# The order list of a three-stage token-mixing kernel, made anew

## The chip, the cores and the metric

The kernel runs on one core of one Trainium2 chip. The metric is the device time of one execution in microseconds. The kernel before takes 290.33 us (median of 3 runs, 290.14 to 290.52).

## The reference

Three layers follow one another on 2 batches of 768 tokens with 512 features, in float32; some weights come as 8-byte floats.

1. Retention attention, 8 heads of 64 features: for each block of tokens, `intra = (q k^T * Dmask) v`, `inter = (q * lam_pow) kv_state`, and then `kv_state = lam_block * kv_state + (k * rev_pow)^T v`.
2. A channel mix: `xk` and `xr` are mixes of each token with the one before it; `k = relu(xk @ w_k)` (512 to 1024), `v = k*k @ w_v`, `r = sigmoid(xr @ w_r)`, and the result is `r * v`.
3. A gated convolution: `gate = sigmoid(sum of 5 shifted, scaled copies of x)`, `val = x @ w_val`, and the output is `(gate * val) @ w_out`.

## The kernel before, in words

All tiles hold 128 partitions. Attention works on 12 chunks of 128 tokens (6 per batch). The two matrix layers work on three passes of 512 tokens (two groups of 256); in every product the operands are split into a high and a low part, and three matmuls (high-high, high-low, low-high) are summed in PSUM. TensorE does all products, VectorE (DVE) and ScalarE (ACT) evict, mix and split, GpSimd (POOL) takes some elementwise work, and SyncE (SP) issues the loads and stores.

Every piece of work is a named operation: `S8` is the scores of chunk 8, `U8` its key-value product, `M8` the masking of the scores on DVE, `N8.0` and `N8.1` the additions to the running state on DVE, `O8.0` and `O8.1` the decay of the state that goes ahead of them, `Y8` and `Z8` the products that make the output, `X8` its eviction. `k1.6.0` is the first half of the sum for row block 6 in pass 1 of the `w_k` product; `r`, `v`, `a` (`w_val`) and `p` (`w_out`) are named alike. `q0`, `k0`, `v0` are loads of tokens, `w0` to `w19`, `y0` to `y3` and `z0` to `z3` loads of weights, and letters behind these (`w3a` to `w3l`) the steps that make two float32 parts of an 8-byte weight.

Nothing plans the work when the kernel is built: one text, `ORDER` (lines 22 to 95), lists all operations, and each is issued in that order on its engine. A letter behind a colon (`:V`, `:A`, `:G`) names another engine than the usual one. An engine does its own operations strictly in the order of the list, and a wait stops all that stands behind it on that engine. A wait is put in where an operation touches what an operation ahead of it in the list has written or read, so the list decides not only when an operation comes, but also for which others it waits.

One PSUM tile matters here, `su`, two banks of 512 columns (line 203). From chunk 4 on, scores and state products share both banks: columns 0 to 255 of each hold what `S` writes and `M` reads, columns 256 to 511 what `U` writes and `N` reads, the first bank for `N.0`, the second for `N.1`:

```
su = psp.tile([P, 2, 512], F32, name="su")                      # line 203
su[half[j], s, Q * n:Q * n + Q]        # S, a matmul, line 571 (Q is 64, s the bank)
su[:, :, 0:NPAIR * Q]                  # M, on DVE, line 578 (NPAIR is 4)
su[half[s], j, c0:c0 + D]              # U, a matmul, line 592 (c0 is 256 + 64 n, j the bank)
u = su[:, j, NPAIR * Q:]               # N, on DVE, line 616
```

`Y` and `Z` are at line 655, all products at 754 and 942. In the trace the 16 or 32 matmul records of an `S` or a `U` stand as one row (`PE su L571`, `PE su L592`); `state` at L616 is an `N`, `b_M` at L578 an `M`.

Of the kernel before, what the change touches and what calls it, by code (L numbers as in the profile page):

```python
# [18 lines left out]


ORDER = """
    zero table eye lam scan warm7 w3 w3b w3a w3c w3d w3e w1 w2 w1a w2a q0 Tq0 w1b warm3 w3f:V
    w3h k0 w1c w1d w2c Tk0 k1 w1e w2d w0 Eq0:A w1f:V kd0 w2b Tk1 w2e w3l:V w2f:V Ek0:A D0:V
    warm2 w0a w0b v0 S0 q1 U0 w1h D1:V w2h k2 N0:A Tq1 w0c q3 pows:G Ek1:A Eq1:A w0d w0e w0f:G
    Tk2 M0 w1l:V S1 Q1 w2l:V Ek2:A D2:G M1 q2 quar Z0 Tq2 O1:V w0h Eq2:A w0l:V Q2 Tq3 Eq3:A Q3
    v1 k3 X0:A U1 N1 S2 Tk3 kd1 Z1 Ek3:A D3:G w4 M2 O2:V w4a X1:A S3 mu w4b muT H0 H1:G w4c
    w4d w4e w4f:G v2 muc mr0.1.0a:A mr0.3.0a:A U2 M3 N2 k4 Tk4 w4h mr0.1.0b mr0.0.0a:A O3:V
    mr0.2.0a:A q4 Z2 X2:A Tq4 mr0.1.0h w4l:V mr0.0.0b v3 mr0.3.0b w5 mr0.2.0b U3 N3 Eq4:A D4:V
    O4.0:V Ek4:A mr0.0.0h mr0.1.0l:V v4 mr0.0.0l:V mr0.3.0h mr0.3.0l:V Z3 Q4 w5a S4 X3:A w5c
    U4 N4.0 O4.1:G r0.00.0 M4 mk0.3a:A mr0.3.1a:A mr0.3.1b k5 Tk5 q5 mr0.1.1a:A Tq5 w5d  # L30
    r0.01.0 mr0.1.1b w5b mr0.0.1a:A mr0.2.0h mr0.0.1b w5e Eq5:A mr0.2.0l:V mk0.0a:A Ek5:A
    mr0.2.1a:A cw0 mk0.0b D5:G mk0.1a:A Y4 mr0.0.1h w7 w7a S5 r0.01.1 N4.1 mr0.1.1h M5
    mr0.2.1b mr0.3.1h mk0.1b w5f:V r0.00.1 mr0.1.1l:V mr0.0.1l:V w6 w6a mr0.3.1l:V w5h w6c w10
# [24 lines left out]
    k1.4.1 k1.5.1 mr1.1l:G k1.2e:V mr1.2a:A O10.0:V k1.2h N10.0 O10.1:G N10.1 Q10:V M10 k1.6.1
    X9:V k11 D11:V k1.1q:V z3 mr1.2b mr1.2h mr1.2l:G r1.3.0 k1.0q:V x1.3:A v11 Y10 S11 k1.4e:A
    k1.4h Z10 X10:A U11 x1.2:A k1.7h mr1.3h O11.0:V N11.0 M11 k1.6e:A k1.1l:V mr1.3l:G k1.6h  # L60
    r1.1.0 k1.2q:V z0 k1.5e:A Y11 Z11 X11:V H5:G r1.2.0 mk2.0a:V x3 mk2.0b r1.2.1 mk2.0h
    r1.3.1 k1.0l:V mk2.1a:V mk2.1b k1.3h k1.3q:A k1.4q:G r1.2s r1.1.1 r1.1s v1.3.0 r1.3s y0
    r1.0.0 r1.0.1 mk2.3a:A v1.0.0 k1.2l:G k1.3l:V v1.3.1 k1.4l:G mk2.2a:V k1.5h y0a mk2.2b
# [1030 lines left out]
```

## Time and profile before

| what | value |
|---|---|
| median of 3 runs | 290.33 us |
| the profiled execution | 290.39 us |
| its span, first to last instruction | 288.6 us |
| PE busy | 275.2 us, 95% |
| DVE busy | 235.4 us, 82% |
| ACT busy | 164.1 us, 57% |
| POOL busy | 49.3 us, 17% |
| granted TensorE clock | 1.000 |

The chain of waits gives PE 90% of the span, DMA 5%, DVE 3%. Busy PE is a modelled figure: matmuls overlap, and the step from one start to the next is what counts. The profiled execution is 1.8 us longer than its span.

### The profile page before, as it was taken

How to read it: one execution, taken by the hardware profiler on the slowest of the kernel's cores; microseconds unless marked ns; L12 is line 12 of the kernel's file. 1: busy time of each engine (PE TensorE's matmuls, PEld its weight loads, DVE VectorE, ACT ScalarE, POOL GpSimd, SP SyncE). 2: the span in 40 equal slices, each digit the busy share in tenths (PEclk: the TensorE clock that was granted, in tenths of full speed). 3: DMA queues.
4: the chain of work that ended last, by engine and by line, in shares of the span. 5: the costliest groups of instructions: out<-in, count | busy, mean ns of one | idle time of the engine just before them, and what ended most of it. 6: DMA issues, size and time to landing. Idle time of an engine off the chain costs nothing.

```text
span 288.6 us, 5971 instructions
## 1 busy us (share of the span) xinstructions
PE 275.2 (95%) x2345; PEld 229.1 (79%) x2345; DVE 235.4 (82%) x402; ACT 164.1 (57%) x309; POOL 49.3 (17%) x59
## 2 busy tenths in 40 slices
...
DMA packets 63626, 29.25 MB, mean 101 GB/s; under 512 B 58322, under 2 KB 58606, under 8 KB 63598
## 3 DMA queue, kind: packets, MB, share of 16 engines
...
q14 instruction: 10, 0.08, 0.1%
HBM read 25.72 MB, written 3.15 MB: 100 GB/s over the span
## 4 chain that ended last, share of the span: by engine, by line
PE 90%; DMA 5%; DVE 3%; ACT 1%; issue 1%; SPq 0%; DVEq 0%; ACTq 0%
PE b_k L754 23%; PE b_v L754 23%; PE b_r L754 12%; PE b_p L942 11%; PE b_a L754 11%; PE xx L655 4%; DMA b_v<-in_v_dram 2%; DMA xx<-in_moe_w_r_dram 2%; PE su L592 2%; PE su L571 1%; PE su L494 1%; PE xx L553 1%; PE b_Tq L440 1%; DVE xx L342 0%; DVE b_k L480 0%
## 5 line engine op out<-in xcount | busy, mean ns | idle before, releaser
L894 DVE SCALAR_TENSOR_TENSOR b_g<-xx,cw,b_g 128x512 f32<-128x512 f32 x48 | 38.5, 810 | 0.6
L754 PE MATMUL b_k<-b_mk_2h,w_rk 128*128 128x512 f32 x48 | 19.0, 397 | 0.0
L754 PE MATMUL b_r<-b_mr_0h,w_rk 128*128 128x256 f32 (+1 forms) x80 | 19.0, 312 | 0.0
L754 PE MATMUL b_k<-b_mk_0h,w_rk 128*128 128x512 f32 x48 | 18.9, 394 | 0.0
L754 PE MATMUL b_k<-b_mk_3h,w_rk 128*128 128x512 f32 x48 | 18.7, 390 | 0.0
L754 PE MATMUL b_k<-b_mk_1h,w_rk 128*128 128x512 f32 x48 | 18.7, 390 | 0.0
L902 ACT ACTIVATE b_g<-b_g 128x512 f32<-128x512 f32 x12 | 7.4, 628 | 16.6 <-DVE b_g L894 16.5
L754 PEld LDWEIGHTS b_r<-b_mr_0h,w_rk 128*128 128x128 f32 x80 | 13.2, 191 | 0.9
L869 DVE TENSOR_TENSOR xx<-b_v,xx 128x512 f32<-128x512 f32 x12 | 8.0, 687 | 6.4 <-PE b_v L754 6.4
L754 PE MATMUL b_r<-b_mr_0l,w_rk 128*128 128x256 f32 (+1 forms) x40 | 12.2, 305 | 0.0
L616 DVE TENSOR_TENSOR state<-su,state 128x256 f32<-128x256 f32 x13 | 5.5, 424 | 6.4 <-PE su L571 3.6
L754 PEld LDWEIGHTS b_k<-b_mk_2h,w_rk 128*128 128x128 f32 x48 | 9.0, 188 | 2.0
L754 PEld LDWEIGHTS b_k<-b_mk_0h,w_rk 128*128 128x128 f32 x48 | 9.0, 188 | 1.9
L754 PEld LDWEIGHTS b_k<-b_mk_3h,w_rk 128*128 128x128 f32 x48 | 9.0, 188 | 1.9
L754 PEld LDWEIGHTS b_k<-b_mk_1h,w_rk 128*128 128x128 f32 x48 | 9.0, 188 | 1.9
L440 PE MATMUL b_Tq<-ident,b_q 128*128 128x128 f32 x24 | 4.3, 309 | 5.6 <-DMA b_q<-in_q_dram 5.6
L754 PE MATMUL b_v<-b_k_0h,w_v 128*128 128x512 f32 x24 | 9.6, 399 | 0.0
L330 ACT ACTIVATE xx<-xx 128x512 int32<-128x512 uint32 x12 | 7.9, 668 | 2.9 <-DMA xx<-in_moe_w_r_dram 2.9
L754 PE MATMUL b_v<-b_k_1h,w_v 128*128 128x512 f32 x24 | 9.4, 391 | 0.0
L754 PE MATMUL b_k<-b_mk_2l,w_rk 128*128 128x512 f32 x24 | 9.4, 390 | 0.0
L754 PE MATMUL b_k<-b_mk_3l,w_rk 128*128 128x512 f32 x24 | 9.4, 390 | 0.0
L754 PE MATMUL b_k<-b_mk_0l,w_rk 128*128 128x512 f32 x24 | 9.4, 390 | 0.0
...
## 6 DMA issues: line engine op xcount, KB each, us to landing
...
```

The costliest lines, as they stand in the source:

```text
L330: op(f"{key}b", "A", lambda e: e.activation(words(I32, 0), words(U32, 0), AF.Copy, scale=2.0 ** -29), reads=[raw], writes=[low])
L440: e.transpose(ps()[:, C * n:C * n + C], src()[:, C * n:C * n + C], ident)
L494: e.matmul(su[:, s, C * n:C * n + C], kt[half[s], n, :], qt[half[s], n, :], start=True, stop=True,)
L553: e.matmul(x[half[b_], a, s, :], w, m, start=a == 0 and kind == (0 if cc else 1), stop=kind == a == 1,)
L592: e.matmul(su[half[s], j, c0:c0 + D], kt[half[j], 2 * n + s if c < PE_CHUNKS else h, :], vt[half[j], h, :], start=True, stop=True,)
L616: op(f"N{c}.{j}", "V", lambda e, u=u, t=state_of[new]: e.tensor_tensor(t, u, t, op=ALU.add), reads=[su_b[f"u{j}"]], writes=[st_b[new]])
L655: last = e.matmul(x[half[b_], j, at, :], w, m, start=spots[i] not in spots[:i], stop=spots[i] not in spots[i + 1:],)
L754: e.matmul(o, r(a), r(b), start=first and n == 0, stop=last and n == len(todo) - 1)
L869: op(f"v{pr}.{rb}e", "V", lambda e: e.tensor_tensor(x2_at(pr, rb), two(ps), x2_at(pr, rb), op=ALU.mult), reads=[ps], writes=[x2_b[pr, rb]])
L894: e.scalar_tensor_tensor(t, src, w, t, op0=ALU.mult, op1=ALU.add)
L902: op(f"g{pr}.{n}s", "A", lambda e: e.activation(acc(), acc(), AF.Sigmoid), writes=[acc])
L942: e.matmul(at(ps), x, w, start=u == 0 and n == 0, stop=u == 1 and n == 5)
```

## The change

Only the text `ORDER` is another one. All operations, their tiles and their code stay; 230 stand on TensorE, as before, while DVE now has 399 (392 before), ACT 298 (304) and POOL 45 (46). A few lines of the list, where the places shown below are:

```diff
-    w6l:V D6:V w10a w10c O5.0:V U5 v6 w9d w8d k0.2.0 w10b w13 k0.0.0 w9e X4:A w11c w13b w11b
+    mk0.3b w5e w9 Ek5:A mk0.0h Y4 Z4 O5.0:V D6:G S5 w7a M5 w6a U5 N5.0 w6c Q5 w6b X4:A w7c v6
...
-    D8:G U8 Bq4 Q8:V D9:V Bk4 S8 N8.0 O8.1:G M8 Y8 N8.1 Z8 O9.0:G mr1.0a:A k1.0e:A k1.0h S9
+    Bk4 N7.1 O8.0:V k1.6.0 U8 N8.0 S8 M8 Y8 k1.4h O8.1:V Z8 X8:A v9 S9 N8.1 U9 O9.0:V mr1.2a:V
```

The rows that follow are the program's own order, with the kind of wait that an instruction has (`DVE_49`: it waits for DVE, `PE_49` for TensorE, `DMAHW...` for a load). Numbers at the end of a name tell buffers apart; `su_77` is the tile `su`.

TensorE at chunks 8 and 9, before: `U8` (L592), `S8` (L571), then `Y8` and `Z8` (L655), of which `b_M8` marks the part that reads the masked scores.

```order
L592 MATMUL su_77<-b_v8_1512,b_k8_1428 64x64 [waits DMAHW1_49,DVE_49,Pool_49]
L592 MATMUL su_77<-b_v8_1512,b_k8_1428 64x64 x15
L571 MATMUL su_77<-b_Bq4_1531,b_Bk4_1536 64x64 [waits DVE_49]
L571 MATMUL su_77<-b_Bq4_1531,b_Bk4_1536 64x64 x15
L655 MATMUL xx_78<-b_Q8_1533,state2_66 64x64 [waits DVE_49]
```

In the list before, no DVE operation on `su` stands between `U8` and `S8`. TensorE at the same place, now:

```order
L592 MATMUL su_77<-b_v8_1506,b_k8_1451 64x64 [waits DMAHW3_49,DVE_49]
L592 MATMUL su_77<-b_v8_1506,b_k8_1451 64x64 x15
L571 MATMUL su_77<-b_Bq4_1508,b_Bk4_1519 64x64 [waits DVE_49]
L571 MATMUL su_77<-b_Bq4_1508,b_Bk4_1519 64x64 x15
L655 MATMUL xx_78<-b_Q8_1510,state2_66 64x64 [waits Pool_49]
```

The three stand in the same order, but in the list now `N8.0` comes between `U8` and `S8`, and `Bk4`, which `S8` reads, has moved ahead of `U8`; `Y8` waits for POOL where it waited for DVE.

DVE at the same place, before: `N8.0`, `M8`, `N8.1`, `N9.0`.

```order
L461 STREAM_TRANSPOSE b_Bk4_1536<-b_jk4_0_1282 128x1024 [waits DMAHW6_49,DMAHW7_49,DMAHW5_49,DMAHW0_49]
L616 TENSOR_TENSOR state2_66<-su_77,state2_66 128x256 [waits PE_49,Pool_49]
L578 TENSOR_TENSOR b_M8_1556<-su_77,dmaskq_61 128x512
L616 TENSOR_TENSOR state0_64<-su_77,state0_64 128x256 [waits Pool_49]
L616 TENSOR_TENSOR state1_65<-su_77,state1_65 128x256 [waits PE_49,Pool_49]
```

In the list before, `N8.0` stands behind `S8`, and `N8.1` ahead of `S9`.

DVE at the same place, now: `N8.0` is the first row with a wait for TensorE, then come `M8`, `N8.1` and `N9.0`, with the decays (L613) between them.

```order
L613 TENSOR_TENSOR state2_66<-state1_65,pw_62 128x256 [waits DVE_49]
L616 TENSOR_TENSOR state2_66<-su_77,state2_66 128x256 [waits DVE_49,PE_49]
L578 TENSOR_TENSOR b_M8_1563<-su_77,dmaskq_61 128x512 [waits PE_49]
L613 TENSOR_TENSOR state0_64<-state2_66,pw_62 128x256 [waits DVE_49]
L616 TENSOR_TENSOR state0_64<-su_77,state0_64 128x256 [waits DVE_49,PE_49]
L613 TENSOR_TENSOR state1_65<-state0_64,pw_62 128x256 [waits DVE_49]
```

In the list now, `N8.0` stands between `U8` and `S8`, and `N8.1` between `S9` and `U9`; `N8.0`, `M8` and `N8.1` have a wait for TensorE each.

TensorE from the second half of `Z8` to the end of `U9`, now (before, the row of `U9` has a wait for its load alone, `DMAHW5_49`):

```order
L655 MATMUL xx_78<-b_M8_1563,b_v8_1506 64x64 [waits DVE_49]
L655 MATMUL xx_78<-b_M8_1563,b_v8_1506 64x64 x15
L571 MATMUL su_77<-b_Bq4_1508,b_Bk4_1519 64x64 x16
L592 MATMUL su_77<-b_v9_1603,b_k9_1414 64x64 [waits DMAHW4_49,DVE_49]
L592 MATMUL su_77<-b_v9_1603,b_k9_1414 64x64 x15
```

`U9` now has a wait for DVE, and in the list `N8.1` is the DVE operation just ahead of it.

TensorE at `U5`, before: the last rows of an `r` product, `U5`, and the first `w_k` product.

```order
L754 MATMUL b_r0_11_0_731<-b_mr0_3_0l_454,w_rk_71 128x256
L754 MATMUL b_r0_11_0_731<-b_mr0_3_0h_452,w_rk_71 128x256
L592 MATMUL su_77<-b_v5_663,b_k5_531 64x64 [waits DMAHW2_49,Pool_49]
L592 MATMUL su_77<-b_v5_663,b_k5_531 64x64 x7
L754 MATMUL b_k0_2_0_803<-b_mk0_0h_665,w_rk_71 128x512 [waits Activation_49]
```

TensorE at `U5`, now: the end of `Z4`, `S5`, `U5`, and an `r` product.

```order
L655 MATMUL xx_78<-b_M4_519,b_v4_442 64x64 x16
L571 MATMUL su_77<-b_Eq5_582,b_Ek5_631 64x64 [waits DVE_49,Activation_49]
L571 MATMUL su_77<-b_Eq5_582,b_Ek5_631 64x64 x15
L592 MATMUL su_77<-b_v5_533,b_k5_448 64x64 [waits DMAHW7_49,DVE_49]
L592 MATMUL su_77<-b_v5_533,b_k5_448 64x64 x7
L754 MATMUL b_r0_10_0_717<-b_mr0_0_0h_424,w_rk_71 128x256 [waits PE_49]
```

`U5` now comes right behind `S5`, with `M5` between them in the list, and has a wait for DVE. Chunk 10 is alike: before, the list has `Y10 S11 Z10 U11`, now `S10 M10 Y10 U11 Z10 S11`.

## Rows read from the trace of the kernel before

**Rows 1.** The page's head: span, and PE's busy time.
```profile
span 288.6 us, 5971 instructions
PE 275.2 (95%) x2345; PEld 229.1 (79%) x2345; DVE 235.4 (82%) x402; ACT 164.1 (57%) x309; POOL 49.3 (17%) x59
```

**Rows 2.** Waits of PE: us in total, times, longest.
```profile
PE b_Tq L440 <- DMA b_q<-in_q_dram: 5.6, 1, 5.6
...
PE xx L655 <- DVE state L616: 0.6, 1, 0.6
...
PE su L592 <- DMA b_v<-in_v_dram: 0.5, 1, 0.5
```

**Rows 3.** Windows: length, busy PE, PEld, DVE, ACT, POOL, clock, DMA share, GB/s.
```profile
5.00:10.00 5.00, 1.34 (x6) 1.03 (x7) 4.86 (x12) 3.72 (x7) 1.66 (x5) 1.00 1.16 317
...
25.00:30.00 5.00, 5.00 (x92) 4.04 (x90) 4.93 (x10) 4.23 (x11) 1.54 (x2) 1.00 1.04 245
...
50.00:75.00 25.00, 24.81 (x260) 19.97 (x261) 24.84 (x47) 22.03 (x42) 3.71 (x4) 1.00 0.67 167
75.00:100.00 25.00, 24.89 (x251) 20.56 (x244) 24.03 (x45) 20.52 (x38) 2.11 (x3) 1.00 0.64 151
...
150.00:175.00 25.00, 25.00 (x112) 20.71 (x111) 19.85 (x40) 10.11 (x19) 5.29 (x4) 1.00 0.00 0
```

**Rows 4.** Timeline of PE, 0 to 45 us: start, duration, what, idle before.
```profile
8.65 1.29 PE L440 MATMUL b_Tq<-ident,b_q 128*128 128x128 f32 x4 [5.61 <-DMA b_q<-in_q_dram]
...
32.81 0.70 PE L592 MATMUL su<-b_v,b_k 64*64 64x64 f32 x32 [0.51 <-DMA b_v<-in_v_dram]
...
37.79 0.69 PE L571 MATMUL su<-b_Eq,b_Ek 64*64 64x64 f32 x32
```

**Rows 5.** The chain that ended last: start, us, what.
```profile
2.11 5.93 DMA xx<-in_moe_w_r_dram
...
25.62 7.06 DMA b_v<-in_v_dram
...
285.62 0.38 ACT b_p_1e L948
```

**Rows 6.** Timeline of PE, 106 to 112 us.
```profile
106.21 0.39 PE L754 MATMUL b_k<-b_mk_3l,w_rk 128*128 128x512 f32 x1
106.43 0.39 PE L754 MATMUL b_k<-b_mk_3h,w_rk 128*128 128x512 f32 x1
106.75 0.70 PE L592 MATMUL su<-b_v,b_k 64*64 64x64 f32 x32
107.27 0.65 PE L571 MATMUL su<-b_Bq,b_Bk 64*64 64x64 f32 x32
108.53 1.03 PE L655 MATMUL xx<-b_Q,state 64*64 64x64 f32 x32 [0.62 <-DVE state L616]
109.38 0.65 PE L655 MATMUL xx<-b_M,b_v 64*64 64x64 f32 x32
109.85 0.65 PE L571 MATMUL su<-b_Bq,b_Bk 64*64 64x64 f32 x32
110.31 0.65 PE L592 MATMUL su<-b_v,b_k 64*64 64x64 f32 x32
110.89 0.50 PE L754 MATMUL b_k<-b_mk_0h,w_rk 128*128 128x512 f32 x1
111.23 0.39 PE L754 MATMUL b_k<-b_mk_0l,w_rk 128*128 128x512 f32 x1
111.46 0.39 PE L754 MATMUL b_k<-b_mk_0h,w_rk 128*128 128x512 f32 x1
```

**Rows 7.** Timeline of DVE, 108 to 112 us.
```profile
108.05 0.42 DVE L616 TENSOR_TENSOR state<-su,state 128x256 f32<-128x256 f32 x1 [1.85 <-PE su L571]
108.39 0.68 DVE L578 TENSOR_TENSOR b_M<-su,dmaskq 128x512 f32<-128x512 f32 x1
...
111.10 0.42 DVE L616 TENSOR_TENSOR state<-su,state 128x256 f32<-128x256 f32 x1 [1.46 <-PE su L592]
```

**Rows 8.** Timeline of DVE near 38.6 us.
```profile
38.62 0.42 DVE L616 TENSOR_TENSOR state<-su,state 128x256 f32<-128x256 f32 x1 [0.58 <-PE su L571]
```

More of the change, by code (lines that the diff above doesn't have):

```diff
@@ L21 @@
 ORDER = """
[L22 to L33, printed above, removed]
@@ L52 @@
-    mk1.2b mk1.1h mk1.1l:V mk1.3h v0.2e v0.3.3 x2.2:A O7.1:G mk1.2h v0.1e k9 v0.0e k1.3.0
-    mk1.3l:V k1.0.0 mk1.2l:V N7.1 O8.0:G v10 k1.3.1 k1.1.0 jq4.2 k1.0.1 jk4.3 jq4.0 jq5.1 v8
-    D8:G U8 Bq4 Q8:V D9:V Bk4 S8 N8.0 O8.1:G M8 Y8 N8.1 Z8 O9.0:G mr1.0a:A k1.0e:A k1.0h S9
-    k1.3e:A jk5.2 U9 N9.0 jq5.3 jq5.0 jq5.2 k1.7.0 k1.1.1 mr1.0b mr1.0h k1.1e:A k1.7.1 M9
-    jk5.0 mr1.1b k1.2.0 k10 k1.2.1 mr1.3a:A Bq5 Q11:V k1.7e:A v0.3e k1.4.0 mr1.3b O9.1:V N9.1
-    jk5.3 D10:V mr1.1h jk5.1 k1.1h k1.6.0 X8:V mr1.0l:V y1 k1.5.0 Q9:V Y9 Z9 U10 Bk5 S10
@@ L58 @@
[L58 to L63, printed above, removed]
@@ L94 @@
-    p5.2.0 p4.1.0 p1.0o a2.3h a2.3l:V p4.0.1 p4.0e:A p2.0e:V p2.0o p2.1o p4.1.1 p4.1e:V p5.2.1
-    p5.0.0 p4.1o p4.0o p5.0.1 p5.2e:V p5.2o p5.0e:A p5.1.0 p5.1.1 p5.1e:A p5.0o p5.1o
+    eye lam zero table H0 scan w3 w2 w3b w3a q0 k0 w2a w3c w3d w3e w0 w2b w1 kd0 w2c w3f:V Tq0
+    Tk0 w3h w2d Eq0:A pows:G Ek0:A warm7 w2e w0a w3l:V w0b S0 w1a q1 w1b warm2 Tq1 Eq1:A k1 k2
+    D0:V w2f:V w2h warm3 Tk1 w0c w0d Ek1:A v0 w0e w1c w0f:G M0 w1d Q1 D1:V Tk2 S1 w1e Ek2:A
+    D2:V w2l:G quar M1 U0 w1f:V q2 w0h Tq2 Eq2:A w4 Z0 N0:A w4a S2 X0:A mu v1 w0l:V w4b k3 w1h
@@ new lines @@
+    Q2 muT w4c O1:V Z1 X1:A w4d w4e w4f:G q3 muc mr0.1.0a:A M2 v2 U1 Tk3 Ek3:A N1 Tq3 D3:V
+    mr0.1.0b Eq3:A mr0.3.0a:A O2:V Q3 mr0.3.0b Z2 S3 mr0.2.0a:A v3 mr0.2.0b U3 w4h kd1 w4l:V
+    U2 mr0.0.0a:A q4 cw0 mr0.3.0h k4 mr0.2.0h mr0.0.0b w1l:G mr0.0.0h M3 mr0.1.0h w5 Tk4 N2
+    Tq4 v4 X2:A mr0.1.0l:V H1:G k5 Z3 D4:V q5 Eq4:A O3:V mr0.3.0l:V Ek4:A S4 mr0.0.0l:V Q4 w6
+    mr0.2.0l:G N3 U4 M4 X3:A mk0.2a:A mk0.2b O4.0:V mr0.1.1a:A mr0.1.1b w5a mr0.0.1a:A
+    mr0.2.1a:A mr0.0.1b v5 mr0.3.1a:A w5c w5b N4.0 r0.00.0 Tk5 D5:V Tq5 w5d mr0.2.1b O4.1:V
@@ new lines @@
+    r0.01.0 mk0.3a:A mr0.1.1h Eq5:A w7 k6 mr0.2.1h mr0.0.1h mr0.3.1b r0.00.1 mr0.2.1l:V
+    mr0.3.1h N4.1 mr0.0.1l:V mr0.3.1l:V mk0.0a:A mk0.0b mr0.1.1l:V r0.01.1 mk0.1a:A r0.01s
+    mk0.3b w5e w9 Ek5:A mk0.0h Y4 Z4 O5.0:V D6:G S5 w7a M5 w6a U5 N5.0 w6c Q5 w6b X4:A w7c v6
+    r0.00s w9a w5f:V mk0.1b w6d w7d r0.10.0 w7b mk0.0l:V r0.11.0 w5h Y5 w6e U6 w5l:V mk0.3h
+    mk0.2h Z5 w11 r0.11.1 mk0.1h mk0.1l:V w7e r0.11s w8 r0.10.1 k0.2.0 N6.0:A w6f:V w6h w9c
+    w7f:V w7h mk0.3l:V jq3.2 w11a w6l:V mk0.2l:V w7l:V w11c w8a w9b w9d r0.10s w8c w10 jq3.1
@@ new lines @@
+    k0.1.0 w9e w11d w8d w11e w8e w10a jq3.3 k0.3.0 k0.3.1 w8b w9f:V w10b w10c w11b k0.3e:A
+    k0.3h k0.3q:A jq3.0 w8f:G Bq3 k0.0.0 w9h w13 w10d k0.0.1 w12 w8h w13a w9l:V w13b w8l:V
+    w10e k0.2.1 k0.3l:V k0.0e:A w11f:V w12a k0.1.1 k0.1e:A w10f:V w11h w12c w13c w10h w12d
+    w13d k0.5.0 w12e w10l:V w11l:V w13e k0.7.0 k0.4.0 k0.2e:A O6.1:V jk3.3 k0.0h k0.2h w12b
+    w12f:V k0.0q:A k0.6.0 k0.5.1 jk3.2 k0.4.1 w13f:V jk3.1 k0.7.1 k0.1h k0.1q:A w13h Q6:G
+    k0.4e:A X5:A jk3.0 Bk3 Y6 k0.5e:A k0.2q:A Q7:V S6 k0.0l:V k7 w15 k0.4h k0.4q:A w14 k0.1l:V
@@ new lines @@
+    w12h D7:G N6.1 M6 v7 k0.2l:V w15a w14a k0.5h k0.6.1 w13l:V w12l:V w15c w14c O7.0:V w14d
+    w15d k0.7e:A Z6 w14e w15e k0.6e:A w16 X6:A w14b w14f:V S7 w17 w16a w16c U7 w15b w14h
+    w15f:G w19 N7.0 w17a H3 w15h M7 jq4.2 w16b w16d w17b w17c w16e v0.1.0 w15l:V w14l:V v0.0.0
+    w16f:V w17d v0.2.0 k0.7h k0.7q:A Y7 w19a Z7 k0.4l:V w17e k0.5q:A H2:G w19c w17f:V w16h
+    w19b v0.3.0 w16l:V w18 w17h k0.5l:V w17l:V v0.0.1 v0.3.1 w18a w18c w18b w19d v0.2.1 w18d
+    jq4.3 k0.6h w19e w18e w19f:V w18f:V X7:A mk1.1a:A v0.1.1 k0.6q:A w18h v0.3.2 v0.0.2 w19h
@@ new lines @@
+    v0.1.2 k0.6l:V jk4.0 k0.7l:V w18l:V w19l:V jq4.0 O7.1:V v0.2.2 jq5.2 mk1.1b mk1.0a:V
+    v0.1.3 mr1.0a:A mk1.2a:A mk1.0b mk1.1h mk1.1l:V mk1.3a:A k9 mk1.3b mk1.0h mk1.0l:V v0.1e
+    v0.3.3 v0.2.3 mk1.3h jk4.3 v0.0.3 mk1.2b mk1.2h mk1.2l:G k8 v0.2e k1.2.0 jk4.2 v0.3e
+    mk1.3l:G v0.0e k1.1.0 k1.4.0 D8:V jk5.1 k1.4.1 k1.4e:A jq4.1 jk4.1 D9:G v8 Bq4 Q8:G k1.5.0
+    Bk4 N7.1 O8.0:V k1.6.0 U8 N8.0 S8 M8 Y8 k1.4h O8.1:V Z8 X8:A v9 S9 N8.1 U9 O9.0:V mr1.2a:V
+    N9.0 k1.6.1 mr1.1a:A k10 O9.1:V k1.1.1 k1.6e:A Q9:V D10:G Y9 jk5.3 v11 M9 mr1.0b H4:A
@@ new lines @@
+    jk5.2 N9.1 k1.6h k1.6q:V mr1.2b Z9 X9:V v10 mr1.1b U10 k1.1e:V mr1.2h x1.1:V k1.5.1 k1.2.1
+    k11 mr1.0h D11:V O10.0:V N10.0 O10.1:V mr1.1h mr1.2l:V k1.4q:V jk5.0 Bk5 k1.5e:A jq5.3
+    mr1.3a:A mr1.1l:G jq5.1 N10.1 mr1.0l:V k1.3.0 k1.7.0 k1.0.0 k1.2e:A k1.7.1 k1.7e:A k1.0.1
+    jq5.0 r1.3.0 k1.3.1 Bq5 mr1.3b mr1.3h k1.1h x2.3:A k1.0e:A Q10:V S10 M10 Y10 U11 y3 Z10
+    k1.3e:V S11 M11 k1.4l:V X10:A mr1.3l:V y1 O11.0:V y1a y1c k1.2h r1.2.0 r1.0.0 r1.1.0 k1.0h
+    N11.0 Q11:V y3a k1.0q:A k1.1q:V k1.0l:G Y11 Z11 r1.3.1 k1.1l:G X11:V z0 z0a H5:A k1.5h
@@ new lines @@
+    r1.0.1 r1.3s r1.0s v1.0.0 k1.2q:G k1.2l:G y1d v1.3.0 mk2.1a:V mr2.0a:V mk2.1b mk2.0a:A
+    k1.3h r1.2.1 k1.3q:A k1.3l:V mr2.3a:V r1.1.1 mk2.2a:V r1.1s k1.5q:V x0 v1.3.1 k1.5l:V
+    x1.2:A k1.6l:G cw cwa cwb cwc cwd cwe cwf:V cwg y3b v1.2.0 mk2.1h mk2.1l:G v1.0.1 r1.2s
+    k1.7h k1.7q:A v1.3.2 k1.7l:V mk2.0b x3 y2 v1.1.0 v1.2.1 v1.2.2 y0 mk2.3a:V mk2.3b v1.2.3
+    v1.1.1 z0b v1.3.3 mk2.2b mk2.0h mk2.2h mr2.3b mk2.2l:V v1.0.2 v1.2e mk2.0l:V y2a y1b y2c
+    v1.1.2 v1.1.3 v1.0.3 v1.3e x1.3:A mk2.3h z0c mk2.3l:G z0d z0e mr2.1a:V k2.3.0 k2.2.0
```

75 lines of the change are left out of this document (28 added, 47 removed).

## The prediction

> **What bounds the kernel now.** I read the page's head first, then the waits of PE, the windows, PE's timeline at the start, the chain, and last PE and DVE side by side where PE waited in mid-kernel. TensorE is busy 275.2 of 288.6 us [rows 1]. Of its idle time, 5.6 us is the wait for the first tokens; a wait of 0.6 us for a state addition (`N8.0`) and one of 0.5 us for a load (`v4`, ahead of `U4`) are the only others to matter here [rows 2]. From 150 us on a window of 25 us holds 25.00 us of PE [rows 3]: there is nothing to win. So the kernel is a start of 32.81 us, which ends when the load of `v4` lets `U4` go [rows 4], a run of matmuls with hardly a gap, and a tail from the last eviction at 285.62 us to the end [rows 5].
>
> This splits the question. I compared what the two lists put on TensorE ahead of `U4`: the same operations, in another order (three warm-ups, five transposes each of q and k, `S0` to `S4`, `U0` to `U3`, `Z0` to `Z3`, one small transpose for the mixing factors). What is left for TensorE from `U4` on is then the same work too. The last product is `p5.1` in both lists, with the larger eviction ahead of it hidden beside that product, so I keep the tail. The time changes by three things only: when `U4` starts, how often TensorE changes between attention and products, and the waits behind `U4`.
>
> **The start.** Before, `q0` is loaded behind three weights, now behind two. A weight is 524,288 bytes; at the 317 GB/s of that window [rows 3] that is 1.65 us, so the first transposes come up to 1.65 us sooner than 8.65 us [rows 4]. But `U4` waits for `v4`, and in both lists the same loads stand ahead of `v4` (six weights, fourteen token loads, `lam` and the mixing factors). The DMA engines are full then (share 1.04, [rows 3]), and `v4` was under way for 7.06 us from 25.62 us on [rows 5]. The same bytes through a full pipe end at nearly the same time. The DVE operations of the list up to `U4`, each at the step its kind has in the trace, sum to 27.6 us now and 28.5 before, so DVE does not hold it back. Bounds: 1.65 us earlier, if all of the lead at `q0` lives on; 0.8 us later, if the loads that were moved ahead of others (`w0`, `w4`) make a chunk's tokens late. I take 0.3 us earlier, near the load's end, since that is what ended the wait in the trace: **-0.3**.
>
> **Changes between attention and products.** One visit to attention inside a run of products costs three longer steps. Going in, the last product takes 106.75 - 106.43 = 0.32 us where its neighbour took 0.22; coming out, `U9` takes 0.58 (110.31 to 110.89) where `S9` took 0.46; and the first product takes 0.34 (110.89 to 111.23) where the next takes 0.23 [rows 6]. Together 0.10 + 0.12 + 0.11 = 0.33 us. Behind `U4` the list before has 12 visits, the new one 10, since `Y4 Z4 S5 U5` and `Y5 U6 Z5` are now in one piece each: 2 x 0.33 = **-0.65**.
>
> **The wait that goes.** `S8` starts at 107.27, `Y8` at 108.53: 1.26 us for a step of 0.46 [rows 6]. It waits for `N8.0`, and `N8.0` started only when `S8` was over, after 1.85 us of idle DVE [rows 7], though it reads what `U8` had written before. The new list has `N8.0` ahead of `S8`, so this wait is gone: **-0.80**.
>
> **The waits that come.** The two facts to read are in rows 7 and 8. `N8.0` waited for `S8`; `N4.1` waited 0.58 us for `S5` [rows 8], which starts at 37.79 [rows 4]. In neither case does the matmul write a column that the addition reads. It shares the bank, and it stands ahead in the list. So what shares `su` is kept in the list's order between TensorE and DVE, columns or not. The new list makes four such pairs where TensorE is the one to wait, and each waits for an addition or a masking that itself waits for the matmuls just ahead.
>
> The pieces: from the start of an `S` or `U` to the start of the DVE operation behind it, 107.27 to 108.05 = 0.78, 110.31 to 111.10 = 0.79, 37.79 to 38.62 = 0.83 [rows 4, 6 to 8]; I take 0.80. From there to the next matmul: 108.05 to 108.53 = 0.48 for an `N` of 0.42, so 0.06 us behind its end, and 0.68 + 0.06 = 0.74 for an `M` [rows 6, 7]. A round over `N` is 1.28 us, over `M` 1.54.
>
> - `U5` behind `M5` behind `S5`: 1.54 instead of a step of 0.46: +1.08.
> - `S8` behind `N8.0` behind `U8`: 1.28 instead of 0.52 (106.75 to 107.27): +0.76.
> - The second part of `Z8` behind `M8` behind `S8`: 1.54 instead of 0.46 + 0.85 (108.53 to 109.38): +0.23.
> - `U9` behind `N8.1` behind `S9`: 1.28 instead of 0.46: +0.82.
> - `U11` behind `M10` behind `S10`: 1.54 instead of 0.46 and a `Y10`. A `Y` is at least half of those 0.85 less some drain; I take 0.37: +0.71.
>
> Sum **+3.60**. The bounds of one such wait are 0, if the DVE wait shown at the instruction is for something long done (at `U5`, the decay `D5`, now on DVE too), and its full round plus what DVE has still to do ahead of it. Behind the waiting `U` stands all of TensorE. They may hide something: while TensorE waits, DVE and ACT catch up.
>
> The Trainium skill (PSUM — Partial Sum Buffer, "PSUM bank collisions raise a hardware error") says that a compiler back end adds a dependency between any two instructions on different engines that touch the same bank in the same group of partitions, whatever the addresses. By that rule all five waits stand; by columns alone only a small part would (third rival). The rows of `N4.1` and `N8.0` are with the rule.
>
> **The rest.** 95 operations move to another engine. Before 95 us DVE is full (24.84 and 24.03 of 25 us, [rows 3]), so I added up what the list gives DVE ahead of the late sums of the first `v` products (`v0.1.3`): 88.9 us now, 89.1 before. Level; I count 0, and DVE loses up to a microsecond waiting for `S5`, while TensorE shifts by as much.
>
> Sum: -0.3 - 0.65 - 0.80 + 3.60 = +1.85 us on the profiled execution's 290.39, so 292.24. That execution is 0.06 above the median; the forecast for the median is **292.2 us**.
>
> **Rivals.**
>
> *DVE becomes late between 50 and 95 us.* It has 7 more operations in all, is full there [rows 3], and now idles for `S5`. For it: one late split of a weight stops a product. Against: its sum up to there is level. A wait of 0.68 us and another like it, and the small work ahead of them, would add about 1.5: 293.7.
>
> *The lead of the start lives on (the other side).* Place: the loads up to `v4`; price: the full 1.65 us in place of my 0.3. It decides the matter if `U4` starts before about 31.5 us: then 292.2 - 1.35 = 290.85, not told from no change. For it: DVE has 0.9 us less to do up to there. Against: the same bytes ahead of `v4`, through full engines.
>
> *The waits do not bite.* If the waits at `U5`, `S8`, `U9` and `U11` are for DVE work long done, what is left is `Y8` behind `N8.0` behind `U8`: 0.80 + 0.48 = 1.28 against 0.52 + 0.46, +0.30. Then -0.3 - 0.65 - 0.80 + 0.30 = -1.45: 288.9. For it: the rows of the order name an engine, not an instruction. Against: rows 7 and 8, where DVE did wait for matmuls of other columns.
>
> **How the numbers follow.** Forecast 0.72, with its own range of 291.2 to 293.2 (the start's bounds cut to the likely part, and 0.1 us at each round); late DVE 0.12; the start's lead 0.10; no waits 0.06. The range of 290.6 to 293.8 leaves out the last rival and the far ends. A measurement of this kernel tells 0.2%, 0.58 us, from no change, so slower begins at 290.91 and faster ends at 289.75. Slower: 0.70 + 0.12 = 0.82. Same: 0.02 of the forecast and 0.08 of the lead, 0.10. Faster: 0.06 and 0.02 of the lead, 0.08.
>
> **What would show it.** In the profile after: PE waits for `b_M` L578 at L592 near 42 and near 128 us, about 1.1 and 0.7 us long; near 107 us waits for `state` L616 at L571 and at L592 of about 0.8 each, and a short one for `b_M` at L655. `U4` (the first L592 row of 32 records) starts between 32.0 and 32.8 us, behind a load. From 150 us on PE is as dense as now. The forecast is wrong if PE's waits behind `U4` sum to less than 2 us, if `U4` starts before 31.5 us, or if PE waits for weights' splits (L348) or loads between 50 and 100 us.

## The result, and the profile after

The kernel now takes 292.61 us (median of 5 runs, 292.01 to 293.63), the kernel before 290.52 beside it. The ratio is 1.0073, with a 95% interval of 1.0046 to 1.0101: slower by 2.1 us. Forecast were 292.2 us, 1.85 more than before. The profiled execution is the fastest of the five, 292.01, and 1.62 above the profiled one of before.

The head of the page, after [rows 1]. PE is not busier, yet the span is longer; in the page's chain of waits PE has 88% and DVE 6%, where they had 90% and 3%.

```profile
span 290.2 us, 5978 instructions
PE 274.3 (95%) x2345; PEld 228.6 (79%) x2345; DVE 239.8 (83%) x409; ACT 160.9 (55%) x303; POOL 62.9 (22%) x58
```

The waits of PE, after: us in total, times, longest [rows 2].

```profile
PE b_Tq L440 <- DMA b_q<-in_q_dram: 7.5, 1, 7.5
PE su L592 <- DVE b_M L578: 1.8, 2, 1.2
...
PE su L571 <- DVE state L616: 0.5, 1, 0.5
PE su L592 <- DVE state L616: 0.5, 1, 0.5
```

The wait of `Y8` (`xx L655` for `state`, 0.6) is gone. Four waits on the tile `su` are new: two of a `U` for an `M`, one of an `S` for an `N`, one of a `U` for an `N`. (`b_Tq` shows 7.5 instead of 5.6 because no warm-up precedes it now.) The windows, after: length, busy PE, PEld, DVE, ACT, POOL, clock, DMA share, GB/s [rows 3].

```profile
50.00:75.00 25.00, 24.89 (x190) 20.42 (x192) 24.50 (x46) 22.52 (x41) 3.65 (x3) 1.00 0.65 185
75.00:100.00 25.00, 24.89 (x239) 20.51 (x229) 24.88 (x48) 20.11 (x35) 10.24 (x3) 1.00 0.51 109
100.00:125.00 25.00, 23.68 (x367) 19.25 (x366) 20.04 (x35) 6.71 (x13) 6.96 (x6) 1.00 0.59 119
125.00:150.00 25.00, 24.15 (x295) 19.65 (x294) 17.29 (x26) 12.12 (x25) 6.43 (x7) 1.00 0.30 109
150.00:175.00 25.00, 25.00 (x112) 20.73 (x111) 19.15 (x36) 10.84 (x19) 3.70 (x4) 1.00 0.00 1
```

PE is full from 150 us on, as before, and as full as before between 50 and 100 us. The holes lie between 100 and 150 us, and one near 42 us. PE's timeline there, after: start, duration, what, idle before [rows 4, 6].

```profile
32.13 0.65 PE L592 MATMUL su<-b_v,b_k 64*64 64x64 f32 x32
32.71 0.39 PE L754 MATMUL b_r<-b_mr_0h,w_rk 128*128 128x256 f32 x1
...
40.83 0.65 PE L571 MATMUL su<-b_Eq,b_Ek 64*64 64x64 f32 x32
42.65 0.68 PE L592 MATMUL su<-b_v,b_k 64*64 64x64 f32 x16 [1.17 <-DVE b_M L578]
...
107.93 0.69 PE L592 MATMUL su<-b_v,b_k 64*64 64x64 f32 x32
109.17 0.69 PE L571 MATMUL su<-b_Bq,b_Bk 64*64 64x64 f32 x32 [0.55 <-DVE state L616]
109.68 0.99 PE L655 MATMUL xx<-b_Q,state 64*64 64x64 f32 x32
110.68 0.69 PE L655 MATMUL xx<-b_M,b_v 64*64 64x64 f32 x32
111.19 0.65 PE L571 MATMUL su<-b_Bq,b_Bk 64*64 64x64 f32 x32
112.38 0.69 PE L592 MATMUL su<-b_v,b_k 64*64 64x64 f32 x32 [0.55 <-DVE state L616]
...
130.32 0.69 PE L571 MATMUL su<-b_Bq,b_Bk 64*64 64x64 f32 x32
130.84 0.41 PE L655 MATMUL xx<-b_Q,state 64*64 64x64 f32 x16
131.90 0.68 PE L592 MATMUL su<-b_v,b_k 64*64 64x64 f32 x16 [0.65 <-DVE b_M L578]
```

These are `U4` and the first product behind it; `S5`, `U5`; `U8`, `S8`, `Y8` with `Z8`, `S9`, `U9`; `S10`, `Y10`, `U11`. DVE beside them, after [rows 7, 8]:

```profile
40.97 0.69 DVE L339 SCALAR_TENSOR_TENSOR b_w5a<-xx,b_w5a 128x512 int32<-128x512 int32 x1
41.57 0.42 DVE L613 TENSOR_TENSOR state<-state,pw 128x256 f32<-128x256 f32 x1
41.91 0.69 DVE L578 TENSOR_TENSOR b_M<-su,dmaskq 128x512 f32<-128x512 f32 x1
...
108.69 0.42 DVE L616 TENSOR_TENSOR state<-su,state 128x256 f32<-128x256 f32 x1 [2.95 <-PE su L592]
109.93 0.69 DVE L578 TENSOR_TENSOR b_M<-su,dmaskq 128x512 f32<-128x512 f32 x1 [0.82 <-PE su L571]
...
111.91 0.42 DVE L616 TENSOR_TENSOR state<-su,state 128x256 f32<-128x256 f32 x1 [0.95 <-PE su L571]
...
131.15 0.69 DVE L578 TENSOR_TENSOR b_M<-su,dmaskq 128x512 f32<-128x512 f32 x1 [2.58 <-PE su L571]
```

Read the two lists together. `N8.0` (108.69) starts 0.76 behind the start of `U8`, and `S8` 0.48 behind the start of `N8.0`. `N8.1` (111.91) waited for `S9`, which writes none of the columns that it reads, and `U9` waited for `N8.1`. (The data need `U9` behind `N8.1`, since it overwrites the columns that `N8.1` reads; they need none of `N8.1` behind `S9`, `S8` behind `N8.0`, `U5` behind `M5` and `U11` behind `M10`.) While one engine works, the other stands: DVE was idle for 0.82 and 0.95 us in this stretch, PE for 0.55 twice.

The first product behind `U4` starts at 32.71 us, 0.73 sooner than the 33.44 of before. From there to the end of the last eviction (287.60, before 286.00) it is 254.89 us, 2.33 more than the 252.56 of before. The sum, +1.60, is the difference of the two profiled executions to 0.02. In this execution `U4` does not wait for the load of `v4`: it starts 0.51 us behind `S4`, with no wait shown.

### The profile page after: what moved, and what is told of

The parts are those of the page before. It is cut to its first block, busy times and chain, and to the rows that moved or that the text cites. A ratio compares the mean times of both kernels' runs of the same rounds, so it can differ in the third digit from the quotient of the medians.

```text
span 290.2 us, 5978 instructions
## 1 busy us (share of the span) xinstructions
PE 274.3 (95%) x2345; PEld 228.6 (79%) x2345; DVE 239.8 (83%) x409; ACT 160.9 (55%) x303; POOL 62.9 (22%) x58
## 3 DMA queue, kind: packets, MB, share of 16 engines
HBM read 25.72 MB, written 3.15 MB: 99 GB/s over the span
## 4 chain that ended last, share of the span: by engine, by line
PE 88%; DVE 6%; ACT 3%; DMA 1%; issue 1%; DVEq 0%; ACTq 0%
PE b_k L754 23%; PE b_v L754 23%; PE b_p L942 11%; PE b_a L754 11%; PE b_r L754 10%; PE xx L655 3%; PE su L592 2%; PE xx L553 2%; PE su L494 1%; PE su L571 1%; DMA b_lam<-in_lam_dram 1%; DVE b_scan L972 1%; ACT w_rk L346 1%; DVE b_mr_0a L734 1%; DVE b_M L578 1%
## 5 line engine op out<-in xcount | busy, mean ns | idle before, releaser
L894 DVE SCALAR_TENSOR_TENSOR b_g<-xx,cw,b_g 128x512 f32<-128x512 f32 x48 | 39.4, 837 | 2.3 <-ACT b_g L896 1.7
L687 POOL COPY b_X<-b_H 128x4 f32<-128x4 f32 x1 | 8.9, 8890 | 4.6 <-DVE b_w17a L339 4.6
L578 DVE TENSOR_TENSOR b_M<-su,dmaskq 128x512 f32<-128x512 f32 x8 | 5.5, 688 | 5.3 <-PE su L571 5.2
```

The source lines that it names most:

```text
L578: op(f"M{c}", "V", lambda e: e.tensor_tensor(pb[c]().rearrange("p (s n) -> p s n", s=2), su[:, :, 0:NPAIR * Q], dmaskq.rearrange("p s n t ...
L687: ) if e is A else e.tensor_copy(xs[g]()[:, :, 0], xs[g - 1]()[:, :, G]),
L894: e.scalar_tensor_tensor(t, src, w, t, op0=ALU.mult, op1=ALU.add)
```

## The experiments

All were timed beside the kernel before. "Rest" is the time from the first product behind `U4` to the end of the last eviction: it leaves the start out, which differs from execution to execution.

| kernel | median, us | ratio to before (95%) | first product, us | rest, us |
|---|---|---|---|---|
| before | 290.5 to 290.6 | | 33.44 | 252.56 |
| changed | 292.61 | 1.0073 (1.0046 to 1.0101) | 32.71 | 254.89 |
| `U5` ahead of `M5` | 291.20 | 1.0029 (1.0008 to 1.0050) | 33.87 | 253.48 |
| `N8.1` early | 291.96 | 1.0047 (1.0034 to 1.0060) | 33.50 | 254.42 |
| `U5` in a visit of its own | 292.56 | 1.0084 (1.0065 to 1.0103) | 32.69 | 255.25 |
| `N4.1` at `U5` | 292.06 | 1.0055 (1.0043 to 1.0067) | 32.97 | 254.23 |
| before, `N8.1` late | 291.31 | 1.0022 (1.0010 to 1.0035) | 33.57 | 253.34 |
| changed, start of before | 292.59 | 1.0064 (1.0048 to 1.0081) | 33.41 | 254.53 |
| before, changed start | 290.60 | 0.9990 (0.9975 to 1.0004) | 34.01 | 252.44 |
| rounds taken apart | 289.80 | 0.9968 (0.9953 to 0.9982) | 34.12 | 251.83 |
| the same, start of before | 289.81 | 0.9974 (0.9965 to 0.9983) | 33.91 | 251.83 |

### U5 ahead of M5

```diff
-    mk0.3b w5e w9 Ek5:A mk0.0h Y4 Z4 O5.0:V D6:G S5 w7a M5 w6a U5 N5.0 w6c Q5 w6b X4:A w7c v6
+    mk0.3b w5e w9 Ek5:A mk0.0h Y4 Z4 O5.0:V D6:G S5 w7a U5 M5 w6a N5.0 w6c Q5 w6b X4:A w7c v6
```

> The changed kernel with one operation moved: in the list U5 stands ahead of M5 instead of behind it. Theory (list order between TensorE and DVE on the tile su makes the wait): U5 no longer waits for DVE, the step from the start of S5 to the start of U5 falls from 1.82 us to about 0.5, and the kernel is about 1.3 us faster than the changed one, about 291.3 us. Rival (the wait was only cover for something later, work on DVE that is late anyway): the step falls, but another wait of PE of about 1 us comes between 43 and 100 us, and the time stays near 292.6. Rival (the wait is for the load of v5 or for other DVE work): the step stays near 1.8.

PE's timeline of this run, `S5` and `U5`:

```profile
41.99 0.65 PE L571 MATMUL su<-b_Eq,b_Ek 64*64 64x64 f32 x32
42.46 0.64 PE L592 MATMUL su<-b_v,b_k 64*64 64x64 f32 x16
```

The step is 0.47 us instead of 1.82, and no wait comes in its place: the rest falls by 1.41 us, the median to 291.20. One operation moved past one other settles it. `U5` and `M5` share no column, so it was the list that made the wait. (They share a bank of `su`; a later run tells bank from tile.)

### N8.1 early

```diff
-    Bk4 N7.1 O8.0:V k1.6.0 U8 N8.0 S8 M8 Y8 k1.4h O8.1:V Z8 X8:A v9 S9 N8.1 U9 O9.0:V mr1.2a:V
+    Bk4 N7.1 O8.0:V k1.6.0 U8 N8.0 S8 M8 Y8 k1.4h O8.1:V N8.1 Z8 X8:A v9 S9 U9 O9.0:V mr1.2a:V
```

> The changed kernel with N8.1 moved ahead of Z8 and S9 in the list (it stood between S9 and U9). Theory: N8.1 runs beside Y8 and Z8 and waits for no matmul of S9; the step from S9 to U9 falls from 1.19 us to about 0.47, 0.7 us less in all, about 291.9. S9 gets a wait for N8.1 in its place, which is long done by then. Rival (the order of columns, not of the list, decides): U9 reads and writes the same columns as N8.1, so the true dependence stays and so does the step of 1.19 us; 292.6.

PE of this run: the second part of `Z8`, `S9`, `U9`.

```profile
111.45 0.69 PE L655 MATMUL xx<-b_M,b_v 64*64 64x64 f32 x32
112.24 0.69 PE L571 MATMUL su<-b_Bq,b_Bk 64*64 64x64 f32 x32
112.75 0.65 PE L592 MATMUL su<-b_v,b_k 64*64 64x64 f32 x32
```

DVE of this run: the decay `O8.1`, then `N8.1`.

```profile
111.31 0.41 DVE L613 TENSOR_TENSOR state<-state,pw 128x256 f32<-128x256 f32 x1
111.76 0.42 DVE L616 TENSOR_TENSOR state<-su,state 128x256 f32<-128x256 f32 x1
```

`U9` is free: 0.51 us behind `S9`. But I had called `N8.1` "long done", and it was not. It stood behind `M8` and `O8.1`, so `S9` came 0.79 us behind `Z8`'s second part instead of 0.51, and part of the gain was lost: 0.47 us of the rest in place of 0.7. That the median, 291.96, is near what was expected is chance: it lies 0.65 us below that of the changed kernel, more than the rest gives. The rival is out, since the step to `U9` did fall though `U9` and `N8.1` share their columns as before.

### U5 in a visit of its own

```diff
-    mk0.3b w5e w9 Ek5:A mk0.0h Y4 Z4 O5.0:V D6:G S5 w7a M5 w6a U5 N5.0 w6c Q5 w6b X4:A w7c v6
-    r0.00s w9a w5f:V mk0.1b w6d w7d r0.10.0 w7b mk0.0l:V r0.11.0 w5h Y5 w6e U6 w5l:V mk0.3h
+    mk0.3b w5e w9 Ek5:A mk0.0h Y4 Z4 O5.0:V D6:G S5 w7a M5 w6a w6c Q5 w6b X4:A w7c v6
+    r0.00s w9a w5f:V mk0.1b w6d w7d r0.10.0 U5 N5.0 w7b mk0.0l:V r0.11.0 w5h Y5 w6e U6 w5l:V mk0.3h
```

> The changed kernel with U5 and N5.0 moved behind the first half of an r product (r0.10.0) in the list; M5 stays ahead of U5. The wait for M5 is then hidden by the product, but U5 makes a visit of its own from the products to attention. Theory (a visit costs about 0.33 us): U5 waits for nothing, and the steps of S5, r0.10.0 and U5 and of the product behind them are 0.3 to 0.35 us more in sum than with U5 right behind S5 and ahead of M5; about 291.6. Rival (a visit costs nothing, the longer steps are given back): the same as that kernel, 291.3.

PE of this run: `S5`, `U5`, `Y5`.

```profile
40.81 0.65 PE L571 MATMUL su<-b_Eq,b_Ek 64*64 64x64 f32 x32
...
43.02 0.68 PE L592 MATMUL su<-b_v,b_k 64*64 64x64 f32 x16
...
46.73 0.46 PE L655 MATMUL xx<-b_Q,state 64*64 64x64 f32 x16 [1.40 <-ACT b_mk_2h L702]
```

DVE of this run: `N5.0`, which now stands behind steps of the weights (L333, L336, L342).

```profile
46.17 0.41 DVE L616 TENSOR_TENSOR state<-su,state 128x256 f32<-128x256 f32 x1
```

The wait for `M5` went and a larger one came. `N5.0` moved with `U5`, past operations of a full DVE, and began 3.15 us behind the start of `U5`; `Y5` reads its state and waited 1.40. The profile puts the wait down to an ACT split that `Y5` does not read (46.05 to 46.66 us); the addition ended at 46.58. So that the wait was for `N5.0` follows from what `Y5` reads, and is not shown by the trace. I had not expected this wait, and the total alone says nothing of the cost of a visit. The steps do: from the start of `S5` to the start of the 24th product matmul behind it is 4.24 us here and 3.88 with `U5` right behind `S5`, 0.36 more, where 0.3 to 0.35 was expected. With the wait of 1.40 that makes 1.76, and the rest of the two kernels differs by 1.77. What moves on TensorE moves its partner on DVE, and most of the price was there.

### N4.1 at U5: bank or tile

```diff
-    mr0.3.1h N4.1 mr0.0.1l:V mr0.3.1l:V mk0.0a:A mk0.0b mr0.1.1l:V r0.01.1 mk0.1a:A r0.01s
+    mr0.3.1h mr0.0.1l:V mr0.3.1l:V mk0.0a:A mk0.0b mr0.1.1l:V r0.01.1 mk0.1a:A r0.01s
-    mk0.3b w5e w9 Ek5:A mk0.0h Y4 Z4 O5.0:V D6:G S5 w7a M5 w6a U5 N5.0 w6c Q5 w6b X4:A w7c v6
+    mk0.3b w5e w9 Ek5:A mk0.0h Y4 Z4 D6:G S5 w7a N4.1 U5 O5.0:V M5 w6a N5.0 w6c Q5 w6b X4:A w7c v6
```

> The changed kernel with U5 ahead of M5, and N4.1 moved from far ahead to between S5 and U5 in the list, with O5.0 behind U5. N4.1 reads the second bank of su only; U5, the last chunk of its batch, writes the first bank only; S5 writes both. If the order is kept bank by bank, U5 has nothing to wait for: S5 to U5 stays about 0.5 us, 291.3 us. If it is kept for the whole tile of two banks, U5 waits for N4.1, which waits for S5: a round of about 1.25 us in place of 0.5, and about 292.1 us.

PE of this run, `S5` and `U5`:

```profile
41.09 0.65 PE L571 MATMUL su<-b_Eq,b_Ek 64*64 64x64 f32 x32
42.28 0.68 PE L592 MATMUL su<-b_v,b_k 64*64 64x64 f32 x16 [0.54 <-DVE state L616]
```

DVE of this run, `N4.1`:

```profile
41.80 0.42 DVE L616 TENSOR_TENSOR state<-su,state 128x256 f32<-128x256 f32 x1
```

`U5` waits for `N4.1`: 1.19 us from `S5`, against 0.47 with the addition out of the way, and 0.75 us more of the rest. The two touch different banks. So in this program the order is kept for the whole tile of two banks. The prediction weighed a rule of the Trainium skill (PSUM — Partial Sum Buffer, "PSUM bank collisions raise a hardware error"), by which a compiler back end adds a dependency where two engines touch the same bank in the same group of partitions. The order here is wider than that rule asks: by it, these two would have been free. For the pairs of the change that meet on `su` both give the same, and the forecast did not hang on it.

### One part alone, in the kernel before

```diff
-    D8:G U8 Bq4 Q8:V D9:V Bk4 S8 N8.0 O8.1:G M8 Y8 N8.1 Z8 O9.0:G mr1.0a:A k1.0e:A k1.0h S9
-    k1.3e:A jk5.2 U9 N9.0 jq5.3 jq5.0 jq5.2 k1.7.0 k1.1.1 mr1.0b mr1.0h k1.1e:A k1.7.1 M9
+    D8:G U8 Bq4 Q8:V D9:V Bk4 S8 N8.0 O8.1:G M8 Y8 Z8 mr1.0a:A k1.0e:A k1.0h S9 N8.1 O9.0:G
+    k1.3e:A jk5.2 U9 N9.0 jq5.3 jq5.0 jq5.2 k1.7.0 k1.1.1 mr1.0b mr1.0h k1.1e:A k1.7.1 M9
```

> The kernel before with one part of the change alone: N8.1 moved from ahead of Z8 to between S9 and U9 in its list, O9.0 (which needs it) right behind it. Theory: the step from S9 to U9 rises from 0.46 us to about 1.2, with a wait for state L616 at U9, and the kernel takes 0.7 us longer, about 291.2. Rival (TensorE has room to catch up, because later work on DVE and ACT sets the time): the step rises and the total stays at 290.5.

PE of this run, `S9` and `U9` [rows 6]:

```profile
109.94 0.65 PE L571 MATMUL su<-b_Bq,b_Bk 64*64 64x64 f32 x32
111.20 0.69 PE L592 MATMUL su<-b_v,b_k 64*64 64x64 f32 x32 [0.61 <-DVE state L616]
```

The step is 1.26 us instead of 0.46, the rest 0.78 longer (253.34 against 252.56), the median 0.7. The 0.80 us that TensorE lost here were not caught up: everything behind moved by about as much.

### The two starts exchanged

The edit puts all that stands ahead of `U4` in the one list in place of that part of the other. The first lines of the changed list with the start of before:

```diff
-    eye lam zero table H0 scan w3 w2 w3b w3a q0 k0 w2a w3c w3d w3e w0 w2b w1 kd0 w2c w3f:V Tq0
...
+    zero table eye lam scan warm7 w3 w3b w3a w3c w3d w3e w1 w2 w1a w2a q0 Tq0 w1b warm3 w3f:V
...
```

> The changed kernel with the list of the kernel before up to U4 (six operations that then stand later than in the changed list follow right behind it: cw0, mr0.2.0h, k5, q5, w6, mr0.2.0l). It measures the start. In five profiles of kernels with the changed start, U4 began at 32.13, 33.17, 32.80, 32.11 and 32.39 us, against 32.81 once before. Theory (the full load pipe gives back most of the lead of 1.1 us that the first tokens have): U4 at about 32.8, rest as in the changed kernel, about 0.3 us slower than it, 292.9, with a smaller spread. Rival (the lead lives on): 1.1 us slower, 293.7.

> The kernel before with the changed list up to U4 (four operations follow right behind it: O4.0, w5a, X3, w5c), the counterpart of the run above. Theory: U4 at about 32.5 on average, 0.3 us faster, about 290.2, with a wider spread of single runs than the 290.1 to 291.5 of the kernel before. Rival (the lead lives on): about 289.4.

Each kernel keeps its time: 292.59 beside 292.61, and a ratio of 0.9990 with an interval (0.9975 to 1.0004) that holds 1. The interval reaches from 0.7 us faster to 0.1 slower: the 0.3 us that I expected is neither shown nor excluded. Over the profiles in the table, with the last two kernels below, the first product comes at 33.58 us on average with the start of before (four, 33.41 to 33.91) and at 33.41 with the changed one (seven, 32.69 to 34.12): a wider spread about nearly the same mean. (Two of the four hold a pause inside `U4`, which the last section shows.) Single times go along: 292.33 to 292.75 with the start of before, 292.01 to 293.63 without. The rival, that the first tokens' lead of 1.1 us lives on, lies outside the interval. Where the lead goes is seen at `S4`, which stands right ahead of `U4` on TensorE; first the kernel before, then the changed one:

```profile
31.61 0.69 PE L571 MATMUL su<-b_Eq,b_Ek 64*64 64x64 f32 x32
31.62 0.70 PE L571 MATMUL su<-b_Eq,b_Ek 64*64 64x64 f32 x32
```

The lead is used up before `U4` has anything to wait for. Part of it went into waits of PE for ACT, DVE and a load between the first tokens and `S4`: 1.55 us in sum in the changed kernel, 0.78 in the one before. Then `v4` can add to that, as in the kernel before with the changed start:

```profile
33.38 0.69 PE L591 MATMUL su<-b_v,b_k 64*64 64x64 f32 x32 [1.03 <-DMA b_v<-in_v_dram]
```

In six of the eleven profiles `U4` comes 0.69 to 1.72 us behind `S4` instead of 0.51 or 0.52, and in each the last of the 16 pieces in which `v4` lands came just before it, at 32.65 to 33.36 us. In the other five, the changed kernel's own among them, that piece was there by 31.93 us and `U4` did not wait. Both kinds occur with both starts. What makes the last piece late is not shown.

### The rounds taken apart

```diff
-    mk0.3b w5e w9 Ek5:A mk0.0h Y4 Z4 O5.0:V D6:G S5 w7a M5 w6a U5 N5.0 w6c Q5 w6b X4:A w7c v6
+    mk0.3b w5e w9 Ek5:A mk0.0h Y4 Z4 O5.0:V D6:G S5 w7a U5 M5 w6a N5.0 w6c Q5 w6b X4:A w7c v6
...
-    Bk4 N7.1 O8.0:V k1.6.0 U8 N8.0 S8 M8 Y8 k1.4h O8.1:V Z8 X8:A v9 S9 N8.1 U9 O9.0:V mr1.2a:V
+    Bk4 N7.1 O8.0:V U8 N8.0 k1.6.0 S8 O8.1:V M8 Y8 k1.4h N8.1 Z8 X8:A v9 S9 U9 O9.0:V mr1.2a:V
...
-    jq5.0 r1.3.0 k1.3.1 Bq5 mr1.3b mr1.3h k1.1h x2.3:A k1.0e:A Q10:V S10 M10 Y10 U11 y3 Z10
-    k1.3e:V S11 M11 k1.4l:V X10:A mr1.3l:V y1 O11.0:V y1a y1c k1.2h r1.2.0 r1.0.0 r1.1.0 k1.0h
+    jq5.0 r1.3.0 Bq5 mr1.3b mr1.3h k1.1h x2.3:A k1.0e:A Q10:V S10 M10 k1.3.1 Y10 U11 y3 Z10
+    S11 k1.3e:V M11 k1.4l:V X10:A mr1.3l:V y1 O11.0:V y1a y1c k1.2h r1.2.0 r1.0.0 r1.1.0 k1.0h
```

> The changed kernel with its rounds between TensorE and DVE taken apart by the list alone: U5 ahead of M5; O8.1 ahead of M8 and N8.1 behind Y8, both ahead of S9; U8 and N8.0 one product half (k1.6.0) earlier; k1.3.1 moved between M10 and Y10. Theory: S5 to U5 1.35 us less, S9 to U9 0.7 less, U8 0.75 less but 0.33 more for a visit of its own, U11 0.78 less but 0.33 more for a visit: 2.9 us less than the changed kernel, about 289.7, faster than the kernel before by 0.8. Rival (a saved wait comes back as another one): between 290.5 and 291.5. The wait at Z8 for M8 (0.15 to 0.25 us) stays.

> The list with the rounds taken apart, now with the start of the kernel before up to U4. In the profiles so far U4 began at 32.81, 32.17 and 32.78 us with the start of before and between 32.11 and 33.50 us, 32.78 on average of seven, with the changed one. Theory (both starts end alike on average, the changed one spreads more): the median stays within 0.3 us of 289.8, U4 near 32.8, single runs spread by less than the 2 us that the other list showed. Rival (the changed start costs its late cases): 0.5 us faster or more, below 289.3.

PE of the first of the two, `U8` to `S9` (between 106.59 and 108.81 the six matmuls of `k1.6.0`, of which the first stands):

```profile
106.59 0.69 PE L592 MATMUL su<-b_v,b_k 64*64 64x64 f32 x32
107.21 0.50 PE L754 MATMUL b_k<-b_mk_0h,w_rk 128*128 128x512 f32 x1
...
108.81 0.69 PE L571 MATMUL su<-b_Bq,b_Bk 64*64 64x64 f32 x32
109.32 0.98 PE L655 MATMUL xx<-b_Q,state 64*64 64x64 f32 x32
110.31 0.69 PE L655 MATMUL xx<-b_M,b_v 64*64 64x64 f32 x32
110.83 0.65 PE L571 MATMUL su<-b_Bq,b_Bk 64*64 64x64 f32 x32
```

Faster than both kernels: 289.80 us, ratio 0.9968 (0.9953 to 0.9982). The rest is 251.83, 3.06 us under the changed kernel; 2.9 was expected. No wait on `su` for DVE is left among PE's waits. With `O8.1` put into DVE's idle time ahead of `M8`, `S9` no longer waits for `N8.1`, and `U9` follows it after 0.47 us. And here the visit is measured: with `U8` on its own, the product ahead and `k1.6.0` behind take 0.09 and 0.14 us longer than in the changed kernel, and `U8` 0.62 instead of the 0.52 of a `U` that waits for nothing [rows 6], 0.33 in sum; with `S10` on its own it is 0.09, 0.14 and 0.11, 0.34.

With the start of before the median is the same, 289.81, with single runs of 289.25 to 290.17 instead of 288.83 to 290.88: what differs is the spread. `U4` near 32.8 us was expected; in the profile it began at 32.15 and then stopped halfway (see the last section).

## Why the prediction was right, point by point

| term | forecast | measured |
|---|---|---|
| start | -0.30 | -0.73 in this execution; over runs not told from none |
| `S8` to `Y8` | -0.80 | -0.74 (1.26 to 0.52) |
| `S5` to `U5` | +1.08 | +1.35 (0.47 to 1.82) |
| `U8` to `S8` | +0.76 | +0.72 (0.52 to 1.24) |
| `Z8`, second part | +0.23 | +0.20 (1.31 to 1.51 from `S8`) |
| `S9` to `U9` | +0.82 | +0.73 (0.46 to 1.19) |
| `Y10` to `U11` | +0.71 | +0.78 (0.28 to 1.06) |
| two visits fewer, and the rest | -0.65 | -0.71 (what is left of +2.33) |

The 0.28 us of a `Y10` ahead of `U11` are read from the kernel before, where `S11` comes next in place of `U11`:

```profile
130.03 0.46 PE L655 MATMUL xx<-b_Q,state 64*64 64x64 f32 x16
130.31 0.65 PE L571 MATMUL su<-b_Bq,b_Bk 64*64 64x64 f32 x32
```

**The bound.** Right: what TensorE loses behind `U4`, the end loses. Each run that gave or took a wait moved the rest by about its size.

**The start.** Half right. The first tokens' lead did not live on, as forecast, but it was gone at `S4` already, in part in waits that the prediction had not looked at. The load of `v4` ended the start in six of eleven profiles, not in all: in the profiled execution `U4` started at 32.13 us, inside the forecast 32.0 to 32.8 but not behind a load. I took 0.3; this execution shows 0.73, and the exchanged starts cannot tell 0.3 from nothing. Without the start the forecast was +2.15, and +2.33 was measured. That the profiled sum, +1.60, comes as near to +1.85 as it does is luck: the start and the rest missed in opposite directions.

**The wait that goes, and the visits.** The first came within 0.06 us of what was read from the rows before. The -0.71 in the line of the visits is a remainder, with all else in it; what shows the 0.33 us of a visit is the last experiment. There are two visits fewer, as counted, but both come from `Y4 Z4 S5 U5`: `Y5`, `Z5` and `U6` stood in one piece before, too.

**The waits that come.** Four of the five stand among PE's waits where they were forecast and for the operation named, 2.92 us in sum (the forecast counted as wrong below 2). Near 107 us PE's idle time is 0.55 us each where 0.8 was named, but the steps grew by 0.72 and 0.73. The fifth, of `Z8` for `M8`, shows no idle time; it is read from its step, and from `M8`, which ends at 110.62, 0.06 us ahead of the second part. Four were sized within 0.1 us. The one mis-sized term is `U5`: a round of 1.54 us was taken, 1.82 measured. `M5` came 1.08 us behind the start of `S5` instead of 0.80, because DVE had a step of a weight (L339) and the decay `O5.0` to do first (40.97 to 41.91 us). The prediction had named this as the upper bound and counted nothing for it.

**The rivals.** *DVE late between 50 and 95 us*: PE is busy for 49.78 us of those two windows, 49.70 before; none of it. *The waits do not bite*: refuted by the rows of `U5` and `U9`, and by the edits that removed them. *The lead lives on*: refuted by the exchanged starts and by the rows of `S4`.

What stays open is why the changed start spreads more. The runs show that it does; its profiles have the last piece of `v4` anywhere between 31.82 and 33.36 us, and no experiment took that apart.
